# A dilated WaveNet convolution: seven wide groups in place of six, another order of blocks, and their preparation in smaller pieces

## Chip, cores and metric

One core of one Trainium2 chip. The metric is the device time of one execution in microseconds (us), the median of several runs. A profile is of one execution; its span runs from the first to the last instruction of the program, and the execution's own time is a little longer than that.

## What is computed

For two sequences of 16,000 steps with 256 channels each, a causal convolution of three taps two steps apart gives 512 channels. The first half goes through tanh, the second through a sigmoid, their product through a 256 x 256 projection. All inputs and the output are bf16.

```python
B, T, D, K = (2, 16000, 256, 3)   # x: B,T,D   w: K,D,2D   w_o: D,D
dil = 2; pad = (K - 1) * dil
xp = jnp.pad(x, ((0, 0), (pad, 0), (0, 0)))
h = einsum('btc,cd->btd', xp[:, pad:pad + T], w[0])
for i in range(1, K):
    off = pad - i * dil
    h = h + einsum('btc,cd->btd', xp[:, off:off + T], w[i])
z = jnp.tanh(h[..., :D]) * sigmoid(h[..., D:])
return z @ w_o
```

## The kernel before

**Tiles.** The 4,000 rows of four steps of each sequence are cut into groups: `groups` (lines 72 to 92), mostly 256 rows (1,024 steps), a few of 160 or 128, and `wides`, groups of 1,024 steps held as 128 rows of eight. A transposing DMA on SP brings x in with channels on partitions: `load_chunk` (line 119) loads two groups at a time into three buffers xt, `load_wide` (line 177) one wide group into two buffers xq. There are 28 plain groups (22 of 256 rows) and six wide ones, three in each sequence. The short groups stand at the end of their sequence: 160 and 128 in the middle of the order, 160, 128 and 128 at its end.

**Fewer products.** Three taps over pairs of steps are computed with fewer matmuls through sums and differences of inputs and of weights, as in a short fast-convolution. A plain block (one group and one of four output tiles of 128 channels) takes four products of two matmuls with 512 columns each: with m and p first (`products`, line 299, `which` 2 and 1), and a block later with d (3 and 0) into the same PSUM banks. Between them ScalarE copies the m product (`copy_m2`, line 338) and VectorE adds it to the p product and subtracts it (`combine`, lines 348 and 349). A wide block nests this twice: 14 matmuls of 256 columns, six at first (`wide_first`, line 232), four behind the preceding block's last products (`wide_second`, line 251) and four in the next block (`wide_last`, line 260). In between come two ScalarE copies (`wide_copies`, lines 241 and 242), two VectorE operations (`wide_sums`, line 247) and two more (`wide_combine`, lines 257 and 258).

**Who prepares.** For a plain group VectorE makes m and p (lines 278 and 284), one each in blocks of output tile 0 and 2, and GpSimd makes d, a quarter a block (`pre_d`, line 295). For a wide group GpSimd makes qa, qb and qd in six parts (`wide_part`, line 199) and, from the second group on, qp (line 214); VectorE makes qm (line 222), and for the first wide group qp also. The wide weights wf, wu and wt come in twelve VectorE steps of 256 columns, three for each output tile (line 571). `after` (line 266) makes each GpSimd operation wait for the last VectorE operation on SBUF in the same block, so that it runs beside the sums that read PSUM.

**The order.** `slots` (lines 497 to 508) lists 136 blocks: plain blocks in order, and from plain block 40 on a wide block behind every two plain ones while all neighbours belong to full groups. The loop (line 597) walks over k. In each block TensorE gets the first products of block k, the last ones of block k - 1, and one piece of the output projection (four matmuls of 256 columns, `out_mm`, line 402) if one is waiting in `todo`; in the last blocks two pieces (line 622). ScalarE gets the copy of block k, the eviction of the piece made in the preceding block (`out_evict`, line 419) and two activations of block k - 1 (`activate`, line 351). VectorE gets `combine(k)`, one of m, p or a gate (line 389), and then the weight steps and the sums of the first wide group that are due in this block. A plain group's pieces enter `todo` in the second block of the next group and may be projected two blocks later. The first wide block is block 40; its twelve half parts stand in every second block from 12 to 34, its weight steps in every second block from 9 to 31, qp in block 35 and qm in block 37. PSUM holds three buffers for each of the two banks a and b of a block, and two for the projection.

Of the kernel before, what the change touches and what calls it, by code (L numbers as in the profile page):

```python
# [9 lines left out]
ALU = mybir.AluOpType  # L10
# [3 lines left out]
def kernel(  # L14
# [57 lines left out]
    groups, chunks, wides = [], [], []  # L72
    for b in range(B):
        r0 = 0
        wide = N_WIDE[min(b, 1)]
        head, tail = sizes(FIRST if b == 0 else (), LAST[min(b, 1)], wide)
        cuts = [1, 1] if b == 0 else []
        for rs in (head, tail):
            i = 0
            while i < len(rs):  # L80
                n = cuts.pop(0) if cuts else 2
                part = rs[i:i + n]
                chunks.append((b, r0, sum(part), len(groups), len(part)))
                for r in part:
                    groups.append(dict(wide=False, b=b, r0=r0, R=r, chunk=len(chunks) - 1, col=r0 - chunks[-1][1]))
                    r0 += r
                i += n
            if rs is head:
                assert r0 > 0 and r0 % 2 == 0
                for _ in range(wide):  # L90
                    wides.append(dict(wide=True, b=b, r0=r0, R=P))
                    r0 += RG
# [93 lines left out]
    def wide_part(n, part, behind=None, qs=slice(0, 2)):  # L186
# [4 lines left out]
        if part == 0 and qs.start == 0:  # L191
            for nm in ("qa", "qb", "qd"):
                G[nm] = q_pool.tile([P, 2, 2, CT, P], bf16, name=nm)
        nm, h, in0, in1, op = (
            ("qa", 0, c[0], c[2], ALU.add), ("qb", 0, e[3], c[1], ALU.add),
            ("qa", 1, c[2], c[0], ALU.subtract), ("qb", 1, e[3], c[1], ALU.subtract),
            ("qd", 0, e[2], c[2], ALU.subtract), ("qd", 1, c[3], e[3], ALU.subtract),
        )[part]
        after(nc.gpsimd.tensor_tensor(out=G[nm][:, h, qs], in0=in0[:, qs], in1=in1[:, qs], op=op), behind)
# [10 lines left out]
    def wide_sum(n, behind=None):  # L210
        G = wides[n]
        G["qp"] = q_pool.tile([P, 2, CT, P], bf16, name="qp")
        eng = nc.gpsimd if SUM_POOL and behind else nc.vector
        ins = eng.tensor_tensor(out=G["qp"][:], in0=G["qa"][:, 0], in1=G["qb"][:, 0], op=ALU.subtract)
        if eng is nc.vector:
            return ins
        after(ins, behind)

    def wide_diff(n):
        G = wides[n]  # L220
        G["qm"] = q_pool.tile([P, 2, 2, CT, P], bf16, name="qm")
        return nc.vector.tensor_tensor(out=G["qm"][:], in0=G["qa"][:], in1=G["qb"][:], op=ALU.add)
# [9 lines left out]
    def wide_first(G, oi):  # L232
        for bank, pool in (("a", ps_a), ("b", ps_b)):
# [5 lines left out]
    def wide_copies(G, oi):  # L239
        G["ss", oi] = ss_pool.tile([P, RG], f32, name="sw")  # L240
        nc.scalar.mul(G["ss", oi][:], G["a", oi][:, RG:], 0.5)
        nc.scalar.mul(G["a", oi][:, RG:], G["a", oi][:, :RG], -1.0)
# [17 lines left out]
    def wide_last(G, oi, bank):  # L260
        if bank == "b":
# [298 lines left out]
    extra = {}  # L560
# [3 lines left out]
    def weight_steps(oi):  # L564
        o = O_ORDER[oi]
        osl = slice(o * P, (o + 1) * P)
        eng = nc.gpsimd if oi in W_POOL else nc.vector

        def tt(out, in0, in1, op):
            def step(last):  # L570
                ins = eng.tensor_tensor(out=out[:, :, osl], in0=in0[:, :, osl], in1=in1[:, :, osl], op=op)
                if eng is nc.vector:
                    return ins
                after(ins, last)
                return last
            return step

        return [
            tt(wf_sb, w_taps[2], w_taps[0], ALU.subtract),
            tt(wu_sb, wf_sb, w_taps[1], ALU.add),  # L580
            tt(wt_sb, wf_sb, w_taps[1], ALU.subtract),
        ]

    steps = [s for oi in range(4) for s in weight_steps(oi)]
    ks = [k for k in range(N_DIRECT + 2, NB) if not slots[k][0]]
    for kk, s in zip([kk for kk in ks if kk >= W_FROM][::W_STEP], steps):
        extra.setdefault(kk, []).append(s)
# [3 lines left out]
    wide_parts = {first_wide - PREP + P_STEP * i: divmod(i, 2) for i in range(12)}  # L591
# [5 lines left out]
    while k <= NB:  # L597
# [3 lines left out]
        if k < NB:  # L601
            if w:
                wide_first(G, oi)
                wide_copies(G, oi)
            else:
                products(k, 2)
                products(k, 1)
                copy_m2(k)
# [8 lines left out]
        if k < NB:  # L617
            for piece in made:
                out_evict(*piece, (not w and g == NG - 1 and oi in (0, 2)) or (len(made) > 1 and piece is made[1]))
            made = []  # L620
        second = (lambda: wide_second(G, oi)) if w else (lambda: wide_last(prev, poi, "b")) if prev["wide"] else None
        n = 0 if k in (NB - 2, NB - 1) else 2 if k > last_wide + 3 and k % 2 and unmade > NB - 1 - k else 1
# [70 lines left out]
        if k in wide_parts:  # L693
            part, q = wide_parts[k]
            wide_part(0, part, last, slice(q, q + 1))
# [9 lines left out]
    assert not todo, len(todo)  # L705
# [31 lines left out]
```

## Time and profile before

| | |
|---|---|
| runs, median (lowest to highest) | 282.95 us (282.88 to 283.25) |
| the profiled execution | 282.88 us |
| its span | 281.1 us |
| mean granted TensorE clock | 0.999 |

In the rows, PE is TensorE, PEld its weight loads, DVE VectorE, ACT ScalarE, POOL GpSimd, SP the engine that issues most DMAs. A row of the timeline has the start in us from the start of the span, the duration in us, engine, line, operation, the tile written <- the tiles read, the shape and how many were merged (x2); in brackets the idle time before it and what ended that. A row of the groups has busy time in us and the mean duration of one in ns behind the bar, then the idle time before them. A row of a stretch has its bounds and length, then for each of PE, PEld, DVE, ACT and POOL the busy time and, in brackets, the number of instructions. An operation's duration is longer than the distance at which the next one can follow, since neighbours overlap: the pace is read from starts.

### The profile page before, as it was taken

Reading aid. Unit: us, or ns where it says so; the run is one execution under the profiler, and the core shown is the slowest. Engines: PE = TensorE matmul, PEld = TensorE weight load, DVE = VectorE, ACT = ScalarE, POOL = GpSimd, SP = SyncE. Lnnn points to the kernel's source line nnn. Section 1 sums busy time; section 2 is a strip of 40 time slices with the busy share of each in tenths; the row PEclk is TensorE's granted clock in tenths of the full one; section 3 lists DMA queues with packets and bytes.
Section 4 is the critical chain, followed back from the end, with each engine's and each line's share of the span. In section 5 each row is a group of like instructions: output and inputs, shape, how many; then the busy total and the mean of one; then the engine's idle time right before and its main releaser. Section 6 shows DMA issues by size and latency. Waiting matters only on the chain.

```text
span 281.1 us, 5263 instructions
## 1 busy us (share of the span) xinstructions
PE 275.2 (98%) x1770; PEld 172.4 (61%) x1770; DVE 262.1 (93%) x477; ACT 260.5 (93%) x553; POOL 148.8 (53%) x160
## 2 busy tenths in 40 slices
PE   8999999999999999999999999999999999999994
PEld 6544555555556665765665666666666666666883
DVE  3999999999999999899999999999999999999994
ACT  5798999999999998999999999999999999999984
POOL 1145756677656663366664766575476553223320
PEclk9999999999999999999999999999999999999999
DMA  8999292642516319536269019515711711222333
GB/s 211 241 192 240 83 219 76 146 123 75 127 75 157 109 45 186 158 119 160 76 137 216 37 40 240 147 40 131 183 40 75 163 40 75 84 74 78 113 124 111
DMA packets 77979, 34.88 MB, mean 124 GB/s; under 512 B 68224, under 2 KB 70144, under 8 KB 77952
## 3 DMA queue, kind: packets, MB, share of 16 engines
q1 hardware_dynamic: 76992, 33.82, 47.4%
q10 hardware_dynamic: 960, 0.72, 0.8%
q8 instruction: 14, 0.23, 0.4%
q14 instruction: 13, 0.11, 0.1%
HBM read 1.18 MB, written 16.38 MB: 62 GB/s over the span
## 4 chain that ended last, share of the span: by engine, by line
PE 92%; DVE 4%; ACT 2%; issue 1%; DVEq 0%
PE b L314 29%; PE a L314 28%; PE o_ps L413 19%; PE a L227 9%; PE b L227 4%; PE a L115 1%; PE a L332 1%; PE b L332 1%; DVE b L348 1%; DVE b L257 1%; DVE a L349 1%; ACT ss L342 1%; ACT thw L362 0%; ACT th L372 0%; DVE mm L278 0%
## 5 line engine op out<-in xcount | busy, mean ns | idle before, releaser
L295 POOL TENSOR_TENSOR dd<-xt 128x512 bf16<-128x512 bf16 (+2 forms) x103 | 99.4, 965 | 110.3 <-DVE zz L389 41.9
L348 DVE TENSOR_TENSOR b<-a,ss 128x512 f32<-128x512 f32 (+2 forms) x108 | 70.0, 649 | 3.7 <-ACT ss L342 1.5
L349 DVE TENSOR_TENSOR a<-a,ss 128x512 f32<-128x512 f32 (+2 forms) x108 | 69.4, 642 | 0.0
L342 ACT COPY ss<-b 128x512 f32<-128x512 f32 (+2 forms) x108 | 60.3, 558 | 9.3 <-PE b L314 2.1
L314 PEld LDWEIGHTS <-wd_sb 128*128 128x128 bf16 x432 | 41.8, 98 | 40.0 <-issue 1.5
L413 PE MATMUL o_ps<-wo_sb,zz 128*128 128x256 bf16 x392 | 63.5, 272 | 0.0
L314 PE MATMUL b<-dd,wd_sb 128*128 128x512 bf16 (+2 forms) x216 | 60.4, 361 | 0.1
L314 PE MATMUL a<-dd,wd_sb 128*128 128x512 bf16 (+2 forms) x216 | 60.4, 361 | 0.0
L314 PE MATMUL a<-pp,wp_sb 128*128 128x512 bf16 (+2 forms) x216 | 60.4, 361 | 0.0
L314 PE MATMUL b<-mm,wm_sb 128*128 128x512 bf16 (+2 forms) x216 | 60.4, 361 | 0.0
L450 ACT CAST osb<-o_ps 128x512 bf16<-128x512 f32 x92 | 55.1, 599 | 0.0
L413 PEld LDWEIGHTS <-zz 128*128 128x128 bf16 x392 | 38.3, 98 | 22.2
L389 DVE TENSOR_TENSOR zz<-th,sg 128x1024 bf16<-128x1024 bf16 (+1 forms) x55 | 37.1, 677 | 0.0
L314 PEld LDWEIGHTS <-wp_sb 128*128 128x128 bf16 x216 | 21.0, 98 | 21.9 <-DVE pp L284 0.7
L372 ACT ACTIVATE sg<-b 128x512 bf16<-128x512 f32 (+2 forms) x56 | 33.0, 589 | 0.9 <-PE b L332 0.5
L372 ACT ACTIVATE th<-b 128x512 bf16<-128x512 f32 (+2 forms) x56 | 32.2, 575 | 1.6 <-PE b L314 0.8
L372 ACT ACTIVATE sg<-a 128x512 bf16<-128x512 f32 (+2 forms) x56 | 33.1, 591 | 0.0
L372 ACT ACTIVATE th<-a 128x512 bf16<-128x512 f32 (+2 forms) x56 | 32.4, 578 | 0.0
L314 PEld LDWEIGHTS <-wm_sb 128*128 128x128 bf16 x216 | 21.0, 97 | 3.5
L257 DVE TENSOR_TENSOR b<-ud,a 128x512 f32<-128x512 f32 x24 | 16.7, 696 | 5.9 <-PE a L227 3.8
L284 DVE TENSOR_TENSOR pp<-xt 128x1024 bf16<-128x1024 bf16 (+2 forms) x27 | 18.2, 673 | 0.0
L247 DVE SCALAR_TENSOR_TENSOR ud<-b,sw 128x256 f32<-128x256 f32 x48 | 17.9, 414 | 0.2
(74 smaller groups left out, 331.2 us busy)
## 6 DMA issues: line engine op xcount, KB each, us to landing
out_dram<-osb SPq DMA_DIRECT2D x60, 256.0 KB, 2.1
w_sb<-in_w_dram ACTq DMA_DIRECT2D x2, 256.0 KB, 4.2
out_dram<-osb_end SPq DMA_DIRECT2D x3, 128.0 KB, 1.9
xn<-in_x_dram SPq DMA_DIRECT2D x1, 256.0 KB, 3.0
w_sb<-in_w_dram SPq DMA_DIRECT2D x1, 256.0 KB, 4.1
xt<-in_x_dram SPq DMA_TRANSPOSE x15, 6.7
wo_sb<-in_w_o_dram ACTq DMA_DIRECT2D x1, 128.0 KB, 5.1
out_dram<-osb_odd SPq DMA_DIRECT2D x8, 16.0 KB, 2.0
```

Source lines behind the costliest of these rows:

```text
L227: nc.tensor.matmul(G[bank, oi][:, half * RG:(half + 1) * RG], lhsT=wmat[:, ct, o * P:(o + 1) * P], rhs=mv[:, :, ct, :], start=first and ct ...
L257: nc.vector.tensor_tensor(out=G["b", oi][:], in0=ud, in1=G["a", oi][:], op=ALU.subtract)
L284: return nc.vector.tensor_tensor(out=G["p"][:, :, :, :G["R"]], in0=xc, in1=yp, op=ALU.add)
L295: ins = eng.tensor_tensor(out=G["d"][:, j, :, :R], in0=a[:, q], in1=s[:, q], op=ALU.subtract)
L314: nc.tensor.matmul(G[bank, oi][:, :N], lhsT=wmat[:, ct, osl], rhs=mv(ct), start=first and ct == 0, stop=ct == CT - 1, skip_group_check=True,)
L342: nc.scalar.copy(out=G["ss", oi][:, :N], in_=G["b", oi][:, :N])
L348: nc.vector.tensor_tensor(out=pb[:, :N], in0=pa[:, :N], in1=ss[:, :N], op=ALU.subtract)
L349: nc.vector.tensor_tensor(out=pa[:, :N], in0=pa[:, :N], in1=ss[:, :N], op=ALU.add)
L372: nc.scalar.activation(out=dst[:, 2 * h:2 * h + 2, :R], in_=G[bank, oi][:, :2 * R].rearrange("p (q r) -> p q r", q=2), func=func, scale=1. ...
L389: return nc.vector.tensor_tensor(out=G["z"][:, dt, :, :full], in0=G["th"][:, dt, :, :full], in1=G["sg"][:, dt, :, :full], op=ALU.mult)
L413: nc.tensor.matmul(o_ps[:, q, :], lhsT=lhsT, rhs=wo_sb[:, dt, :], start=(dt == 0), stop=(dt == NT - 1),)
L450: copy(out=osb[:, 2 * jp:2 * jp + 2, :], in_=o_ps[:])
```

## The change

There are seven wide groups, four of them in the first sequence, and so 27 plain groups (21 of 256 rows). With `SHORT_LAST` the short groups of the first sequence go to the end of the order, ahead of those of the second: the last five groups have 160, 128, 160, 128 and 128 rows. `SPACING` says for every wide block how many plain blocks stand ahead of it: the first wide block is now block 31 and its group's others are 33, 40 and 43; from block 49 to 112 the distances repeat as 2, 1, 2, 2. Spelt out by the loop above, that is (W a wide block, its group and tile; the numbers are plain group and tile):

```
31 W0.0  32 7.3   33 W0.1  34 8.0 ... 39 9.1   40 W0.2  41 9.2  42 9.3  43 W0.3  44 10.0 ... 48 11.0
49 W1.0  50 11.1  51 W1.1  52 11.2  53 11.3  54 W1.2  55 12.0  56 12.1  57 W1.3  58 12.2  59 12.3  60 W2.0 ...
104 W6.0  105 20.0  106 W6.1  107 20.1  108 20.2  109 W6.2  110 20.3  111 21.0  112 W6.3  113 21.1 ... 135 26.3
```

The first wide group's six parts come as 24 quarters in the blocks of `P_AT` (two quarters of one half in the same block are one operation, so blocks 23 and 29 have a half), its weight steps as 24 halves in the blocks of `W_AT` (both halves in one block are one operation), all on VectorE; qp in block 19, qm in block 24. Two pieces are projected in block 126 alone; the piece evicted in blocks 9 and 129 goes to VectorE. `HOLD`, `COPIES`, `W_ENG` at these values leave the rest as it was: a wide block's two copies are still ahead of the eviction on ScalarE.

```diff
-    N_WIDE = (3, 3)
-    WIDE_FROM = 40
-    PREP = 28
-    W_FROM = 9
-    EVERY = (2,)
-    W_POOL = ()
+    N_WIDE = (4, 3)
+    SPACING = (31, 1, 6, 2, 5, 1, 2, 2, 2, 1, 2, 2, 2, 1, 2, 2, 2, 1, 2, 2, 2, 1, 2, 2, 2, 1, 2, 2,)
+    W_ENG = (0, 0, 0, 0, 0, 0, 0, 0, 0, 0, 0, 0)
+    W_AT = (6, 6, 10, 10, 14, 14, 16, 17, 18, 18, 22, 22, 24, 25, 26, 26, 28, 29, 30, 30, 34, 36, 38, 38)
+    P_AT = (7, 10, 10, 11, 12, 13, 14, 15, 16, 17, 18, 19, 20, 21, 23, 23, 23, 24, 25, 26, 27, 28, 29, 29)
+    SUM_AT, DIFF_AT = 19, 24
+    HOLD = ()
+    TWICE = (126,)
+    COPIES = 0
+    EVICT_DVE = (9, 129)
+    SHORT_LAST = True
...
+        ends.append(tail)
+        if not SHORT_LAST or b == B - 1:
+            for e in range(b + 1 if SHORT_LAST else 1):
+                add_groups(e if SHORT_LAST else b, ends[e if SHORT_LAST else b])
...
-        after(nc.gpsimd.tensor_tensor(out=G[nm][:, h, qs], in0=in0[:, qs], in1=in1[:, qs], op=op), behind)
+        after(nc.gpsimd.tensor_tensor(out=G[nm][:, h, qs, cts], in0=in0[:, qs, cts], in1=in1[:, qs, cts], op=op), behind)
...
-        if rest and i + 1 >= WIDE_FROM and since >= EVERY[(4 * len(wides) - len(rest)) % len(EVERY)] and full:
+        if rest and since >= SPACING[4 * len(wides) - len(rest)] and full:
...
-    wide_parts = {first_wide - PREP + P_STEP * i: divmod(i, 2) for i in range(12)}
+    wide_parts = {}
+    for i, kk in enumerate(P_AT):
+        wide_parts.setdefault(kk, []).append((i // 4, i % 4))
...
+            if w and COPIES == 0:
+                wide_copies(G, oi)
             for piece in made:
-                out_evict(*piece, (not w and g == NG - 1 and oi in (0, 2)) or (len(made) > 1 and piece is made[1]))
+                out_evict(*piece, (not w and g == NG - 1 and oi in (0, 2)) or (len(made) > 1 and piece is made[1]) or k in EVICT_DVE)
...
-        n = 0 if k in (NB - 2, NB - 1) else 2 if k > last_wide + 3 and k % 2 and unmade > NB - 1 - k else 1
+        n = 0 if k in (NB - 2, NB - 1) or k in HOLD else 2 if k in TWICE else 1
...
-        if k == first_wide - 5:
+        if k == SUM_AT:
             last = wide_sum(0)
-        if k == first_wide - 3:
+        if k == DIFF_AT:
             last = wide_diff(0)
 
-        for step in extra.get(k, ()):
-            last = step(last)
+        steps = extra.pop(k, [])
+        for i in sorted({i for i, _ in steps}):
+            cts = [ct for j, ct in steps if j == i]
+            last = weight_step(i, slice(cts[0], cts[-1] + 1), last)
```

More of the change, by code (lines that the diff above doesn't have):

```diff
@@ L72, with add_groups @@
     groups, chunks, wides = [], [], []
+    starts = [0] * B
+    def add_groups(b, rs, cuts=()):
+        cuts, i = list(cuts), 0
+        while i < len(rs):
+            n = cuts.pop(0) if cuts else 2
+            part = rs[i:i + n]
+            chunks.append((b, starts[b], sum(part), len(groups), len(part)))
+            for r in part:
+                col = starts[b] - chunks[-1][1]
+                groups.append(dict(wide=False, b=b, r0=starts[b], R=r, chunk=len(chunks) - 1, col=col))
+                starts[b] += r
+            i += n
+    ends = []
     for b in range(B):
-        r0 = 0
         wide = N_WIDE[min(b, 1)]
         head, tail = sizes(FIRST if b == 0 else (), LAST[min(b, 1)], wide)
[L77 to L92, printed above, removed]
+        add_groups(b, head, [1, 1] if b == 0 else [])
+        assert starts[b] > 0 and starts[b] % 2 == 0
+        for _ in range(wide):
+            wides.append(dict(wide=True, b=b, r0=starts[b], R=P))
+            starts[b] += RG
+        ends.append(tail)
+        if not SHORT_LAST or b == B - 1:
+            for e in range(b + 1 if SHORT_LAST else 1):
+                add_groups(e if SHORT_LAST else b, ends[e if SHORT_LAST else b])
+    assert starts == [T // 4] * B
     XW = max(c[2] for c in chunks)
@@ L184, in load_wide, with wide_part @@
         )
-    def wide_part(n, part, behind=None, qs=slice(0, 2)):
+    def wide_part(n, part, behind=None, qs=slice(0, 2), cts=slice(0, CT)):
         G = wides[n]
@@ L211, in wide_sum @@
         G = wides[n]
+        assert all(G["made", part] == 2 * CT for part in (0, 1))
         G["qp"] = q_pool.tile([P, 2, CT, P], bf16, name="qp")
@@ L220, in wide_diff @@
         G = wides[n]
+        assert all(G["made", part] == 2 * CT for part in (0, 1, 2, 3))
         G["qm"] = q_pool.tile([P, 2, 2, CT, P], bf16, name="qm")
@@ L232, in wide_first @@
     def wide_first(G, oi):
+        assert all(w_made.get(3 * oi + i) == CT for i in range(3))
         for bank, pool in (("a", ps_a), ("b", ps_b)):
@@ L260, in wide_last @@
     def wide_last(G, oi, bank):
+        assert all(G["made", part] == 2 * CT for part in (4, 5))
         if bank == "b":
@@ L557, with weight_step @@
     drain(groups[0], N_DIRECT + 2)
-    extra = {}
+    extra, w_made = {}, {}
     last_wide = max(k for k in range(NB) if slots[k][0])
     first_wide = slots.index((True, 0, 0))
[L564 to L587, printed above, removed]
+    for i, kk in enumerate(W_AT):
+        extra.setdefault(kk, []).append((i // 2, i % 2))
+    def weight_step(i, cts, last):
+        o = O_ORDER[i // 3]
+        sl = (slice(None), cts, slice(o * P, (o + 1) * P))
+        out, in0, in1, op = (
+            (wf_sb, w_taps[2], w_taps[0], ALU.subtract),
+            (wu_sb, wf_sb, w_taps[1], ALU.add),
+            (wt_sb, wf_sb, w_taps[1], ALU.subtract),
+        )[i % 3]
+        assert i % 3 == 0 or w_made.get(3 * (i // 3)) == CT
+        w_made[i] = w_made.get(i, 0) + cts.stop - cts.start
+        eng = nc.gpsimd if W_ENG[i] else nc.vector
+        ins = eng.tensor_tensor(out=out[sl], in0=in0[sl], in1=in1[sl], op=op)
+        if W_ENG[i]:
+            after(ins, last)
+            return last
+        return ins
     load_wide(0)
     wides_loaded = 1
-    wide_parts = {first_wide - PREP + P_STEP * i: divmod(i, 2) for i in range(12)}
+    wide_parts = {}
+    for i, kk in enumerate(P_AT):
+        wide_parts.setdefault(kk, []).append((i // 4, i % 4))
     held = []
@@ L704 @@
         k += 1
-    assert not todo, len(todo)
+    assert not todo and not extra and not wide_parts, len(todo)
     finish(made)
```

29 lines of the change are left out of this document (22 added, 7 removed).

## Prediction

> **What bounds the kernel now.** I read the page's busy times first, then the chain of work that ended last, then TensorE's instructions in order of time, and last VectorE and GpSimd where TensorE waits.
>
> ```profile
> PE 275.2 (98%) x1770; PEld 172.4 (61%) x1770; DVE 262.1 (93%) x477; ACT 260.5 (93%) x553; POOL 148.8 (53%) x160
> PE 92%; DVE 4%; ACT 2%; issue 1%; DVEq 0%
> ```
>
> The span is 281.1 us. TensorE (PE) owns 92% of the chain, but VectorE (DVE) and ScalarE (ACT) are busy for 93% each: there are three nearly full engines, and whoever falls behind stops TensorE. A busy PE says little about its pace, so I take the pace from the starts of blocks: the first matmul of a plain block reads mm, that of a wide block reads qp.
>
> ```profile
> 27.70 0.59 PE L314 MATMUL b<-mm,wm_sb 128*128 128x512 bf16 x2
> 57.99 0.38 PE L314 MATMUL b<-mm,wm_sb 128*128 128x512 bf16 x1
> 159.62 0.27 PE L227 MATMUL a<-qp,wm_sb 128*128 128x256 bf16 x1
> 184.80 0.27 PE L227 MATMUL a<-qp,wm_sb 128*128 128x256 bf16 x1
> ```
>
> The first two rows start blocks 13 and 27: 14 plain blocks in 30.29 us, 2.164 us each. The last two start blocks 78 and 90, the second blocks of wide groups 2 and 3: 8 plain and 4 wide blocks in 25.18 us, so a wide block takes (25.18 - 8 x 2.164) / 4 = 1.968 us. A wide block issues 18 matmuls of 256 columns with its piece of the output projection (14 + 4), so one costs 0.109 us; a plain block issues 8 of 512 and 4 of 256, so one of 512 costs 0.216 us.
>
> How much does TensorE lose? I count the matmuls between the starts of blocks 5 and 135.
>
> ```profile
> 11.20 0.38 PE L314 MATMUL b<-mm,wm_sb 128*128 128x512 bf16 x1
> 273.73 0.38 PE L314 MATMUL b<-mm,wm_sb 128*128 128x256 bf16 x2
> ```
>
> The code issues 700 of 512 columns, 904 of 256 and 64 of 320 there (0.136 us, between the two others): 151.1 + 98.8 + 8.7 = 258.6 us at the pace above. The rows are 262.5 us apart, so **about 4.0 us is stall**. Within this stretch a better order cannot win more than that, beyond fewer matmuls. The largest losses, as starts of neighbouring blocks:
>
> ```profile
> 22.97 0.59 PE L314 MATMUL b<-mm,wm_sb 128*128 128x512 bf16 x2
> 25.54 0.38 PE L314 MATMUL b<-mm,wm_sb 128*128 128x512 bf16 x1
> ...
> 104.29 0.27 PE L227 MATMUL a<-qp,wm_sb 128*128 128x256 bf16 x1
> 106.60 0.38 PE L314 MATMUL b<-mm,wm_sb 128*128 128x512 bf16 x1
> 108.81 0.38 PE L314 MATMUL b<-mm,wm_sb 128*128 128x512 bf16 x1
> ...
> 130.27 0.38 PE L314 MATMUL b<-mm,wm_sb 128*128 128x512 bf16 x1
> 132.29 0.38 PE L314 MATMUL b<-mm,wm_sb 128*128 128x512 bf16 x1
> ...
> 149.43 0.38 PE L314 MATMUL b<-mm,wm_sb 128*128 128x512 bf16 x1
> 151.17 0.38 PE L314 MATMUL b<-mm,wm_sb 128*128 128x512 bf16 x1
> ...
> 155.29 0.38 PE L314 MATMUL b<-mm,wm_sb 128*128 128x512 bf16 x1
> 157.46 0.38 PE L314 MATMUL b<-mm,wm_sb 128*128 128x512 bf16 x1
> ```
>
> Against its matmuls, block 11 is 0.41 late (2.57 against 2.16); block 49 0.35 (2.31 against 1.96: wide, no projection piece); block 50 0.47 (2.21 against 1.74: a plain block behind a wide one); block 64 0.28 (2.02 against 1.74); block 73 0.44 (1.74 against 1.30: no piece); block 76 0.43 (2.17 against 1.74). That is 2.38 of the 4.0. Counting the pieces through the queue of the code, blocks 48, 49, 62, 73 and 74 have none to project: TensorE runs 0.44 us ahead in each, and DVE and ACT, with nearly as much work as ever, do not follow. (43 and 54 have none either, without a loss of note.) Five of the six losses sit at these or within two blocks behind.
>
> **The change, part by part.** The sum is made against the profiled execution, 282.88 us: 281.1 of span and 1.78 around it. The median of the runs, 282.95, is 0.07 higher.
>
> *A seventh wide group.* It replaces one plain group: 32 matmuls of 512 columns go and 56 of 256 come, 6.91 - 6.12 = **0.79 us less** on the path. DVE pays more for a wide block:
>
> ```profile
> 148.75 0.74 DVE L247 SCALAR_TENSOR_TENSOR ud<-b,sw 128x256 f32<-128x256 f32 x2
> 149.60 0.70 DVE L257 TENSOR_TENSOR b<-ud,a 128x512 f32<-128x512 f32 x1
> ```
>
> The two ud operations hold it for 0.85 us, two sums of 0.60 follow, and three gates or sums of 0.60 fall on the four blocks: some 2.5 us a block. At 7 plain blocks of 1.80 (worked out below) to 4 wide ones that is 22.6 us of DVE in 7 x 2.164 + 4 x 1.968 = 23.0 of TensorE: it fits, with 0.4 to spare, so I cost it at nothing.
>
> *Short groups at the end, one wide block in 2.8.* The five short groups do the same work at the end, where the pieces (one each block, two in block 126) never run out until block 134; the last three groups and the 7.4 us behind row 273.73 stay. By the same count the new order has no piece in blocks 8 to 10 as now, then only in 35, 36, 45 and 46, each two plain blocks behind a wide one, and none from 47 to 133. So the five losses behind block 48 have lost their cause: **1.97 us less**. I put 0.2 back for 35, 36, 45 and 46 (bounds: nothing, and 0.44 each by block 73's row).
>
> *First weight step from block 9 to 6.* Block 11's loss is a wait for the sum of block 10, which stands behind that step:
>
> ```profile
> 19.05 0.70 DVE L348 TENSOR_TENSOR b<-a,ss 128x512 f32<-128x512 f32 x1 [0.18 <-ACT ss L342]
> ...
> 23.00 0.41 DVE L571 TENSOR_TENSOR wf_sb<-w_sb 128x256 f32<-128x256 bf16 x1
> 23.33 0.69 DVE L348 TENSOR_TENSOR b<-a,ss 128x512 f32<-128x512 f32 x1
> ```
>
> Taking it out starts that sum 0.33 us earlier. At block 6 it is partly covered: DVE waits 0.18 us for ACT ahead of 19.05 anyway. That leaves 0.15 of the step and the first GpSimd (POOL) piece, now in block 7, which together take back some 0.2. I take **0.13 less** (0 to 0.4). Evicting on DVE in block 9 does nothing, since no piece is made in block 8. In block 129 one eviction goes from ACT to DVE:
>
> ```profile
> L450 DVE CAST osb<-o_ps 128x512 bf16<-128x512 f32 x4 | 2.7, 684 | 0.0
> ```
>
> Four such stand among the last short blocks now and two then (another behind block 126), so I cost it at nothing.
>
> *Preparation over blocks 6 to 38.* This is the disputed part. Twelve weight steps on DVE and the first wide group's sums on POOL have to be done by block 31 for the most part, not by 40. What a POOL piece costs DVE is in these rows:
>
> ```profile
> 50.29 0.68 DVE L284 TENSOR_TENSOR pp<-xt 128x1024 bf16<-128x1024 bf16 x1
> ...
> 52.10 1.17 DVE L389 TENSOR_TENSOR zz<-th,sg 128x1024 bf16<-128x1024 bf16 x1
> ```
> ```profile
> 51.05 1.04 POOL L295 TENSOR_TENSOR dd<-xt 128x512 bf16<-128x512 bf16 x1 [0.76 <-DVE pp L284]
> 52.05 0.67 POOL L199 TENSOR_TENSOR qa<-xq 128x256 bf16<-128x256 bf16 x1
> L199 POOL TENSOR_TENSOR qa<-xq 128x512 bf16<-128x512 bf16 x10 | 11.5, 1154 | 0.0
> ```
>
> From one SBUF operation to the next DVE has pp and the two sums, three operations in 1.81 us, 0.60 each: 1.80 for a plain block. POOL's difference dd fills the two sums, which read PSUM. The half piece behind it begins 0.05 us before DVE's gate, and the gate takes 1.17 us where pp took 0.68: a half costs DVE 0.49 us. A half takes 0.67 us and a full one 1.15, so a quarter takes about 0.42 (an estimate from these two), and costs 0.49 - 0.25 = 0.24, less where POOL comes second or DVE is waiting: I take 0.20 (bounds: nothing, and the 0.49 of a half).
>
> Now DVE from block 12 to 30 of the new order: 19 blocks at 1.80 make 34.3; weight steps, five whole at 0.33 (from 23.00 to 23.33) and six halves at about 0.2, 2.9; the two sums of wide group 0 at 0.33 and 0.60, 0.9; sixteen quarters 3.2 and two halves 0.9. Together 42.2 us. TensorE needs 19 x 2.164 = 41.1. So DVE is 1.1 us late by block 31; a little of that TensorE does not feel, since DVE may fall somewhat further behind than it is at block 12, and I take **1.0 us more** (bounds: quarters at 0.13 or less, no stall; at 0.49, 4.6 us more than this). The rest of the steps, blocks 34 to 38, is 0.7 us of DVE where wide blocks stand six apart.
>
> *Transfers and the other queues.* The load of wide group 0 stays ahead of the loop; the order of chunk and wide loads on SP changes, but each later wide load is again issued in a wide group's last block, at least two plain blocks before the next group. I cost this at nothing; if one came late, POOL's sums and then a wide group's first matmuls would be late with it.
>
> **The sum:** -0.79 - 1.97 + 0.2 - 0.13 + 1.0 = -1.7 us. **282.88 - 1.7 = 281.2 us.**
>
> **The rivals.** *The quarters hide.* If POOL's quarters cost DVE 0.13 or less, the ledger above closes and the 1.0 goes: 280.2. For it: 0.05 us decides in the rows whether the piece or the gate comes first, and behind the gate a quarter would lie beside the sums. Against, with less preparation per block now:
>
> ```profile
> 37.70:81.90 44.20, 44.20 (x248) 23.86 (x247) 44.20 (x72) 42.12 (x83) 29.56 (x31) 1.00 0.43 114
> ```
>
> The third time is DVE's: busy for all of 44.2 us.
>
> *The missing pieces stall TensorE as now.* Blocks 35, 36, 45 and 46 lose 0.44 each, 1.8 in all, not 0.2: 282.8, no measurable difference. That is also what it would come to if the shorter order only moved its stalls. Against: they stand second and third behind a wide block, not at it.
>
> *The close pair.* The second block of each wide group now follows the first after one plain block, not two: seven times wide, plain, wide. ACT's copies decide there:
>
> ```profile
> 105.24 0.47 ACT L241 ACTIVATE sw<-a 128x256 f32<-128x256 f32 x1
> ...
> 147.67 0.39 ACT L241 ACTIVATE sw<-a 128x256 f32<-128x256 f32 x1
> ...
> 148.85 0.61 ACT L372 ACTIVATE th<-b 128x512 bf16<-128x512 f32 x1
> 149.34 0.62 ACT L372 ACTIVATE th<-a 128x512 bf16<-128x512 f32 x1
> ```
>
> In block 49 (start 104.29) the first copy began 0.95 us after the block, and block 49 lost 0.35; in block 72, whose successor starts at 149.43 and which takes 2.39 us, it began 0.63 after, with no loss. In the close pair I work out 0.82: ACT's four operations of 0.48 (148.85 to 149.34) exceed the plain block's 1.74 us by 0.18. If 0.82 is already too late, seven pairs at 0.35 cost 2.5 us, and with block 50's 0.47 behind each 5.7: 283.7 to 286.9, **slower**. It decides from a copy that begins some 0.9 us late. Against: the second block has no gate on DVE, and 0.1 us is left.
>
> *Pieces block for their whole length.* If a quarter, begun 0.05 us ahead, holds the gate until it ends, it costs 0.37, and sixteen of them add 2.7 us to a full DVE: 283.9; with the 0.49 of a half 285.8. Slower, from 0.34 a quarter on. Against: the half in the rows would have cost 0.62 so, and cost 0.49. The Trainium skill ("SBUF — State Buffer", Who interferes with whom) says that a VectorE operation with two SBUF inputs and a GpSimd operation that reads SBUF shut each other out for the whole instruction. By that rule this rival is what comes; the trace bears out the blocking, not its full length.
>
> **How the numbers follow.** Forecast 0.52; quarters hide 0.30; missing pieces 0.08; close pair 0.05; whole length 0.05. A measurement can tell about 0.2% (0.57 us) from no change, so faster means below 282.4 and slower above 283.5: faster 0.82, the same 0.08, slower 0.10. The range takes in the second case, down to 279.4 with 0.3 from block 11 and 0.5 from the 1.6 us of smaller losses not listed, and the missing pieces, up to 282.8.
>
> **What would show it.** Right: plain periods of 2.164 and wide ones of 1.968 throughout blocks 50 to 112, with DVE idle for almost nothing from 25 to 70 us and TensorE's blocks 12 to 31 together some 1.0 us late; POOL's quarters near 0.42 us, gates of 0.9 behind them. The first loss at block 11 shrinks to 0.2 to 0.3. Wrong: late blocks at every second wide block (the pair), or gates as long as 1.17 behind quarters, or short blocks at the end that take longer than 1.31 us (128 rows, with a piece).

## The result, and the profile after

The changed kernel takes **280.44 us** (median, 280.27 to 280.68); the kernel before, in the same comparison, 283.07. The ratio is 0.9908 with a 95% interval of 0.989 to 0.9925: faster by 0.9%. The forecast was 281.2, with a range of 279.4 to 282.8. The profiled execution took 280.49 us against 282.88. First the span, the busy times and the chain of work that ended last, from the page of the changed kernel:

```profile
span 278.7 us, 5344 instructions
...
PE 273.5 (98%) x1794; PEld 175.8 (63%) x1794; DVE 262.3 (94%) x486; ACT 260.4 (93%) x559; POOL 155.6 (56%) x173
...
PE 90%; DVE 8%; issue 1%; DVEq 0%
```

From this page little has changed: TensorE issues 24 matmuls more and is busy 1.7 us less, and VectorE has taken some of the chain from ScalarE. Where the time went is seen in the starts of blocks, in TensorE's timeline of the changed kernel (the first matmul of a plain block reads mm, that of a wide block qp; "..." marks rows left out):

```profile
11.66 0.59 PE L336 MATMUL b<-mm,wm_sb 128*128 128x512 bf16 x2
...
25.39 0.59 PE L336 MATMUL b<-mm,wm_sb 128*128 128x512 bf16 x2
...
55.68 0.59 PE L336 MATMUL b<-mm,wm_sb 128*128 128x512 bf16 x2
58.17 0.59 PE L336 MATMUL b<-mm,wm_sb 128*128 128x512 bf16 x2
...
67.06 0.38 PE L243 MATMUL a<-qp,wm_sb 128*128 128x256 bf16 x2
69.98 0.59 PE L336 MATMUL b<-mm,wm_sb 128*128 128x512 bf16 x2
72.33 0.38 PE L243 MATMUL a<-qp,wm_sb 128*128 128x256 bf16 x2
...
104.75 0.38 PE L243 MATMUL a<-qp,wm_sb 128*128 128x256 bf16 x2
...
236.49 0.38 PE L243 MATMUL a<-qp,wm_sb 128*128 128x256 bf16 x2
...
271.56 0.38 PE L336 MATMUL b<-mm,wm_sb 128*128 128x256 bf16 x2
```

These start blocks 5, 12, 26, 27, 31, 32, 33, 49, 112 and 135. From 5 to 135 it is 259.90 us. The matmuls between them need about 257.8 at the pace of the prediction, so the stall is 2.1 us; before it was about 4.0 of 262.53. Blocks 49 to 111, 40 plain and 23 wide, need 86.6 + 45.3 = 131.8 us and take 131.74: the middle of the kernel loses nothing. Block by block, the losses of the changed kernel are

| block | 6 | 10 | 11 | 26 | 28 | 31 | 32 | 41 |
|---|---|---|---|---|---|---|---|---|
| us | 0.14 | 0.07 | 0.10 | **0.32** | **0.20** | **0.53** | **0.61** | 0.09 |

Blocks 35, 36, 45 and 46, which have no piece to project, lose nothing; so do the close pairs. The four losses in bold, 1.66 us, are the end of the preparation. Two stretches there, blocks 12 to 25 and 26 to 32, each with its length and the busy time of PE, PEld, DVE, ACT and POOL:

```profile
25.40:55.68 30.28, 30.28 (x170) 16.42 (x168) 30.25 (x50) 28.55 (x57) 23.84 (x29) 1.00 0.62 142
55.68:72.33 16.65, 16.14 (x93) 8.68 (x90) 16.55 (x30) 14.71 (x30) 11.79 (x15) 1.00 0.27 84
```

VectorE is as full in the first stretch (30.25 of 30.28), which loses nothing, as in the second, which loses 1.66. A full engine is not yet a late one. How late it is shows in the distance from a block's first matmul to VectorE's first sum of that block: 1.99 us in block 12, still only 1.35 in block 24 (from 51.35 to 52.70), and 2.45 in block 25 (from 53.52 to 55.97). So VectorE does not fall behind little by little: up to block 24 it catches up. Between the sums of blocks 24 and 25, where mm, qm, half a weight step and the pieces beside them come together (the rows stand under e4), it loses 1.1 us at once, and from there to its first ud of block 31 another 1.0 (13.95 us for six blocks of 2.164).

### The profile page after: what moved, and what is told of

Its sections match the earlier page's. It is cut to its first block, busy times and chain, and to the rows that moved or that the text cites. A ratio compares the mean times of both kernels' runs of the same rounds, so it can differ in the third digit from the quotient of the medians.

```text
span 278.7 us, 5344 instructions
## 1 busy us (share of the span) xinstructions
PE 273.5 (98%) x1794; PEld 175.8 (63%) x1794; DVE 262.3 (94%) x486; ACT 260.4 (93%) x559; POOL 155.6 (56%) x173
## 4 chain that ended last, share of the span: by engine, by line
PE 90%; DVE 8%; issue 1%; DVEq 0%
PE b L336 27%; PE a L336 27%; PE o_ps L435 18%; PE a L243 11%; PE b L243 4%; DVE b L370 2%; DVE a L371 2%; PE a L354 1%; PE a L128 1%; DVE zz L411 1%; PE b L354 1%; DVE pp L306 1%; DVE wt_sb L601 0%; DVE wf_sb L601 0%; DVE qm L238 0%
## 5 line engine op out<-in xcount | busy, mean ns | idle before, releaser
L317 POOL TENSOR_TENSOR dd<-xt 128x512 bf16<-128x512 bf16 (+2 forms) x99 | 95.2, 962 | 101.8 <-DVE zz L411 32.9
L370 DVE TENSOR_TENSOR b<-a,ss 128x512 f32<-128x512 f32 (+2 forms) x104 | 67.3, 648 | 3.8 <-ACT ss L364 1.5
L371 DVE TENSOR_TENSOR a<-a,ss 128x512 f32<-128x512 f32 (+2 forms) x104 | 66.7, 641 | 0.0
L336 PE MATMUL b<-dd,wd_sb 128*128 128x512 bf16 (+2 forms) x208 | 58.0, 360 | 0.2 <-DVE b L370 0.2
L336 PE MATMUL a<-dd,wd_sb 128*128 128x512 bf16 (+2 forms) x208 | 58.0, 360 | 0.0
L336 PE MATMUL a<-pp,wp_sb 128*128 128x512 bf16 (+2 forms) x208 | 58.0, 361 | 0.0
L411 DVE TENSOR_TENSOR zz<-th,sg 128x1024 bf16<-128x1024 bf16 (+1 forms) x53 | 34.3, 649 | 0.0
L278 DVE TENSOR_TENSOR b<-ud,a 128x512 f32<-128x512 f32 x28 | 19.5, 696 | 4.0 <-PE a L243 1.9
L268 DVE SCALAR_TENSOR_TENSOR ud<-b,sw 128x256 f32<-128x256 f32 x56 | 20.9, 413 | 0.1
L435 PE MATMUL o_ps<-wo_sb,zw 128*128 128x256 bf16 x112 | 19.6, 273 | 0.0
```

Source lines behind the costliest of these rows:

```text
L268: nc.vector.scalar_tensor_tensor(out=G["ud", oi][:, h], in0=G["b", oi][:, RG:], scalar=0.5, in1=G["ss", oi][:], op0=ALU.mult, op1=op)
L278: nc.vector.tensor_tensor(out=G["b", oi][:], in0=ud, in1=G["a", oi][:], op=ALU.subtract)
L317: ins = eng.tensor_tensor(out=G["d"][:, j, :, :R], in0=a[:, q], in1=s[:, q], op=ALU.subtract)
L336: nc.tensor.matmul(G[bank, oi][:, :N], lhsT=wmat[:, ct, osl], rhs=mv(ct), start=first and ct == 0, stop=ct == CT - 1, skip_group_check=True,)
L370: nc.vector.tensor_tensor(out=pb[:, :N], in0=pa[:, :N], in1=ss[:, :N], op=ALU.subtract)
L371: nc.vector.tensor_tensor(out=pa[:, :N], in0=pa[:, :N], in1=ss[:, :N], op=ALU.add)
```

## The experiments

All are edits of the parameters of the changed kernel; e4 also adds a few lines of code. Where "..." stands in an edit, lines are left out. After each label stands the edit, then what was expected, then what came out. "Loss" is the time of a block over what its matmuls need; times are medians, and ratios are to the kernel before, run on the same chip.

**e1: only the short groups at the end.** The number of wide groups, their places and their preparation go back to what they were; one piece is projected in every block to the end, where the kernel before has two in some of the last blocks.

```diff
-    N_WIDE = (4, 3)
-    SPACING = (31, 1, 6, 2, 5, 1, 2, 2, ...)
-    W_AT = (6, 6, 10, 10, 14, 14, 16, 17, ...)
-    P_AT = (7, 10, 10, 11, 12, 13, ...)
-    SUM_AT, DIFF_AT = 19, 24
-    TWICE = (126,)
-    EVICT_DVE = (9, 129)
+    N_WIDE = (3, 3)
+    SPACING = (40,) + (2,) * 23
+    W_AT = (9, 9, 11, 11, ..., 31, 31)
+    P_AT = (12, 12, 14, 14, ..., 34, 34)
+    SUM_AT, DIFF_AT = 35, 37
+    TWICE = ()
+    EVICT_DVE = ()
```

> The kernel before with one part of the change alone: the short groups of the first sequence moved to the end, one piece projected in every block to the end, no eviction moved; six wide groups from block 40 on, every third block, preparation where it was. By count only blocks 43, 48 and 49 then have no piece to project. Theory A (TensorE loses its time where no piece is left to project and VectorE and ScalarE cannot follow): the 0.8 us of blocks 49 and 50 stay, the 1.15 of blocks 64, 73 and 76 and some 0.5 of the short blocks go: 283.0 - 1.65 = 281.4 us (281.1 to 281.8). Rival B (the gain came from the seventh group and the earlier start, and the losses merely go elsewhere): 283.0 within 0.3.

Measured 281.37 us, 0.9937 (0.9914 to 0.996). Blocks 11, 49 and 50 lose 0.40, 0.35 and 0.48 as they did; the losses behind block 50, of blocks 64, 73, 76 and 97 and of the short blocks at the end, are gone but for 0.16 in the last blocks. So this order, with one piece in each of the last blocks, brings about two thirds of what the whole change brings.

**e4: no pieces on GpSimd.** The first wide group's parts are not made; its tiles are set to zero ahead of the loop, so that group's output leaves out its input.

```diff
-    P_AT = (7, 10, 10, 11, 12, 13, ...)
+    P_AT = ()
+        wides[0][nm] = q_pool.tile([P, 2, 2, CT, P], bf16, name=nm)
+        nc.gpsimd.memset(wides[0][nm][:], 0.0)
...
```

> The changed kernel without GpSimd's sums of the first wide group, whose tiles are set to zero at the start (that group's output leaves out its input). Theory A (GpSimd's pieces and VectorE's weight steps together overfill VectorE before block 31): the losses of blocks 26, 28, 31 and 32, 1.7 us, go: 278.8 (278.5 to 279.2). Rival B (the weight steps and the first wide block's own waits make them): less than 0.5 of it goes, 279.9 or more.

Measured 278.87 us, 0.9855 (0.9838 to 0.9873), and blocks 26, 28, 31 and 32 lose nothing. The weight steps stand where they stood, and the same VectorE operations are short. VectorE's timeline around block 26, first of the changed kernel, then of e4:

```profile
43.48 0.93 DVE L411 TENSOR_TENSOR zz<-th,sg 128x1024 bf16<-128x1024 bf16 x1
...
52.70 0.69 DVE L370 TENSOR_TENSOR b<-a,ss 128x512 f32<-128x512 f32 x1
...
53.90 1.13 DVE L300 TENSOR_TENSOR mm<-xt 128x1024 bf16<-128x1024 bf16 x1
54.96 0.88 DVE L238 TENSOR_TENSOR qm<-qa,qb 128x1024 bf16<-128x1024 bf16 x1
55.77 0.28 DVE L601 TENSOR_TENSOR wf_sb<-w_sb 128x128 f32<-128x128 bf16 x1
55.97 0.68 DVE L370 TENSOR_TENSOR b<-a,ss 128x512 f32<-128x512 f32 x1
...
68.54 1.12 DVE L306 TENSOR_TENSOR pp<-xt 128x1024 bf16<-128x1024 bf16 x1
69.58 0.41 DVE L601 TENSOR_TENSOR wf_sb<-w_sb 128x256 f32<-128x256 bf16 x1
69.92 0.74 DVE L268 SCALAR_TENSOR_TENSOR ud<-b,sw 128x256 f32<-128x256 f32 x2
70.76 0.70 DVE L278 TENSOR_TENSOR b<-ud,a 128x512 f32<-128x512 f32 x1
```
```profile
54.14 0.69 DVE L305 TENSOR_TENSOR mm<-xt 128x1024 bf16<-128x1024 bf16 x1
54.74 0.68 DVE L243 TENSOR_TENSOR qm<-qa,qb 128x1024 bf16<-128x1024 bf16 x1
55.34 0.29 DVE L606 TENSOR_TENSOR wf_sb<-w_sb 128x128 f32<-128x128 bf16 x1
...
67.12 0.69 DVE L311 TENSOR_TENSOR pp<-xt 128x1024 bf16<-128x1024 bf16 x1
```

The pieces that stood beside them in the changed kernel, on POOL:

```profile
43.44 0.43 POOL L213 TENSOR_TENSOR qa<-xq 128x128 bf16<-128x128 bf16 x1
...
53.85 0.63 POOL L213 TENSOR_TENSOR qb<-xq 128x256 bf16<-128x256 bf16 x1
54.44 0.85 POOL L213 TENSOR_TENSOR qd<-xq 128x128 bf16<-128x128 bf16 x1
...
68.50 0.61 POOL L213 TENSOR_TENSOR qd<-xq 128x256 bf16<-128x256 bf16 x1
```

A quarter of 0.43 us that begins 0.04 ahead of the gate makes the gate 0.93 in place of the 0.68 that gates take in e4; a half of 0.63, 0.05 ahead of mm, makes it 1.13. That is 0.25 and 0.45, about 0.18 less than the piece lasts. Most quarters do cost what the prediction said, and do not hide. A few cost nothing: the one at 48.03, behind a gate that begins at 47.93, has two sums after it, and the first of them begins 0.62 us after the gate.

**e2: halves in place of quarters**, and **e3: six wide groups in place of seven**, the order otherwise as in the change.

```diff
-    P_AT = (7, 10, 10, 11, 12, 13, ...)
+    P_AT = (7, 7, 9, 9, 11, 11, ..., 29, 29)
```
```diff
-    N_WIDE = (4, 3)
+    N_WIDE = (3, 3)    # and the last group's four distances cut from SPACING
```

> The changed kernel with the first wide group's sums as twelve halves in every second block from 7 to 29 in place of the smaller pieces. Theory A (a piece costs VectorE its time beyond the sums that read PSUM: 0.49 us a half, 0.24 a quarter, so twelve halves cost 5.9 and the twenty quarters and two halves 5.8): 280.4 within 0.4, blocks 12 to 32 lose 1.2 to 2.2 us. Rival B (small pieces are what lets the preparation fit): at least 1 us slower, 281.4 or more.

> The changed kernel with six wide groups in place of seven, the order otherwise the same up to block 101. Theory A (TensorE sets the pace from block 44 on, so the seventh group is worth its matmuls): 0.79 us more, 281.2 (281.0 to 281.5). Rival B (VectorE sets the pace in the wide stretch, so fewer matmuls save nothing there): 280.4 within 0.2, or less.

e2 measured 280.9 us, 0.9928 (0.9909 to 0.9947), between the two answers. Blocks 26 to 32 lose 1.36 in place of 1.66, but blocks 11 and 12, now beside halves, lose 0.35 and 0.47 and blocks 20 to 24 another 0.2. So the halves spare VectorE nothing: 0.3 less is lost there, and some 0.9 more ahead of it.

e3 measured 281.81 us, 0.9956 (0.9944 to 0.9968), with a spread of 281.42 to 282.38; that is above both answers (the first reached to 281.5). In its trace the matmuls need 0.79 more, as expected, blocks 26 to 32 lose the same, and only block 5 differs much, by 0.36. Of the 1.4 us between the two medians 0.8 is thus the seventh group; where the other 0.6 comes from is open (block 5's 0.36 can be a part of it).

**e7: wide blocks at every third place**, and **e8: the close pair moved by one wide block**, so that its second block is the group's third.

```diff
-    SPACING = (31, 1, 6, 2, 5, 1, 2, 2, 2, 1, 2, 2, ...)
+    SPACING = (31,) + (2,) * 27
```
```diff
-    SPACING = (31, 1, 6, 2, 5, 1, 2, 2, 2, 1, 2, 2, ...)
+    SPACING = (31, 1, 6, 2, 5, 2, 1, 2) + (2, 2, 1, 2) * 5
```

In e7 half a weight step also moved from block 34 to 35, since 34 is now a wide block.

> The changed kernel with the wide blocks at even distance, every third block from 31 to 112 with no close pair (step 10 in blocks 35 and 36). Theory A (the close pair costs nothing; a block without a piece costs about 0.44 us where it stands directly behind a wide block): blocks 35 and 41 now stand so, and 0.7 to 0.9 us is added there: 281.2 us (280.9 to 281.6), with no change from block 49 on. Rival B (the close pairs cost something that the even order saves): 280.4 or less.

> The changed kernel with the close pair of wide groups 1 to 6 moved from their first and second block to their second and third, where VectorE has a gate in the third. Theory A (the pair is free only where its second block has no gate): in the third block VectorE's sum starts 2.76 us after the block's start in place of 2.57, so each of six pairs loses about 0.2: 1.2 us more, 281.6 (281.2 to 282.0). Rival B (a close pair is free anywhere): 280.4 within 0.2.

e7 measured 282.61 us, 0.9988 (0.9974 to 1.0002), worse than either answer. It loses 2.1 us more in blocks 35 to 44 and nothing from 49 on. So the close pair is no cost, and the prediction's empty blocks cost nothing because they stand two or three behind a wide block: put directly behind one, as blocks 35 and 41 here, they cost 0.24 and 0.74. (The profiled execution, 281.9, is 0.7 below the median; that rest is open.)

e8 measured 281.75 us, 0.9956 (0.9942 to 0.9969). Each of the six moved pairs loses 0.20 or 0.21, everything else as in the change. The first of them, blocks 54 to 56 on TensorE, and the sum of wide block 54 on VectorE:

```profile
115.10 0.38 PE L243 MATMUL a<-qp,wm_sb 128*128 128x256 bf16 x2
117.49 0.59 PE L336 MATMUL b<-mm,wm_sb 128*128 128x512 bf16 x2
119.43 0.59 PE L336 MATMUL b<-mm,wm_sb 128*128 128x512 bf16 x2
```
```profile
117.87 0.70 DVE L278 TENSOR_TENSOR b<-ud,a 128x512 f32<-128x512 f32 x1
```

Block 55 takes 1.94 us where its matmuls need 1.74, and the sum of block 54 began 117.87 - 115.10 = 2.77 us after its block. This is the number that ties the cases together, below.

**e5: the weight steps of the other output tiles later**, behind the first wide block, and wide block 2 one place later; **e6: the first wide block at 34**, with all pieces single quarters; **e9 and e11: the weight steps moved alone**, e9 partly ahead of the first wide block, with qm in block 27, e11 behind it as e5, but in the order of the change.

```diff
e5  SPACING = (31, 1, 6, 3, 4, 1, 2, 2, ...)
e5  W_AT = (6, 6, 10, 10, 14, 14, 16, 17, 18, 18, 22, 22, 32, 32, 34, 34, 37, 37, 30, 30, 38, 38, 41, 41)
e6  SPACING = (34, 1, 4, 2, 4, 1, 2, 2, ...)
e6  W_AT = (6, 6, 10, 10, 14, 14, 18, 18, 22, 22, 26, 26, 30, 30, 32, 32, 35, 35, 37, 37, 38, 38, 42, 42)
e6  P_AT = (7, 10, 11, 12, ..., 31, 32)
e6  SUM_AT, DIFF_AT = 19, 27
e9  W_AT = (..., 22, 22, 23, 23, 25, 25, 32, 32, 30, 30, 34, 34, 38, 38)
e9  SUM_AT, DIFF_AT = 19, 27
e11 W_AT = (..., 22, 22, 28, 28, 32, 32, 34, 34, 30, 30, 37, 37, 38, 38)
```

> The changed kernel with weight steps 6 to 8 (counted from 0) moved from blocks 24 to 29 to blocks 32, 34 and 37, step 10 from 34 and 36 to 38, step 11 from 38 to 41, and the fourth wide block from 43 to 44. Theory A (VectorE is overfilled by some 1.5 us ahead of block 31, and any 1.1 us taken out of blocks 24 to 30 comes back on TensorE): the losses of blocks 26 to 32, 1.7 us, fall to 0.6 and nothing of note is added behind: 279.4 us (279.1 to 279.8). Rival B (only GpSimd's pieces matter, since a run without them lost nothing with all weight steps in place): less than 0.4 is won, 280.0 or more.

> The changed kernel with the first wide group at blocks 34, 36, 41 and 44 in place of 31, 33, 40 and 43; its pieces as 24 single quarters in block 7 and blocks 10 to 32, weight steps whole in blocks 6, 10, 14, 18, 22, 26, 30, 32, 35, 37, 38 and 42, the second sum in block 27. Theory A (the ledger of VectorE: 22 blocks from 12 to 33 hold 47.4 us of work in 47.6 of TensorE's): the losses of 1.7 us ahead of the first wide blocks shrink to under 0.5, some 0.2 is lost at blocks 39 to 41: 279.2 us (278.9 to 279.8). Rival B (the first wide block itself costs what blocks 31 and 32 lose, wherever it stands): 1.1 us stays there, 280.0 or more.

> The changed kernel with weight steps 6, 7 and 8 in blocks 23, 25 and 32 (whole), step 10 whole in block 34, and wide group 0's second sum in block 27 in place of 24; the order of blocks untouched. Theory A (the losses ahead of block 33 are one overfull stretch of VectorE, so it is enough to spread the same work by the room that each block has): of the 1.7 us some 0.1 stays at block 31, nothing is added: 278.9 us (278.7 to 279.3). Rival B (the wide start itself has a price that only a later fourth wide block or fewer pieces takes away): 279.6 or more.

> The changed kernel with its order of blocks untouched (fourth wide block at 43, second sum in block 24) and weight steps 6 to 11 whole in blocks 28, 32, 34, 30, 37 and 38: as in the run with later weight steps, but with one step back ahead of block 31 and none behind block 40. Theory A (room on VectorE block by block): block 26 loses 0.13 as there, block 31 or 32 some 0.2, blocks 36, 37 and 41 together 0.4, block 45 nothing since it no longer stands directly behind a wide block: 279.1 us (278.9 to 279.5). Rival B (the order of the balanced run's miss: anything added ahead of block 31 comes back whole): block 32 loses 0.5 or more, 279.6 or more.

| | us | ratio (95%) | stall, 5 to 135 | losses that remain |
|---|---|---|---|---|
| e5 | 279.22 | 0.9866 (0.984 to 0.9891) | 1.14 | 26 0.13, 41 0.23, 45 0.37 |
| e6 | 280.15 | 0.99 (0.9875 to 0.9925) | 1.77 | 41 0.28, 42 0.44, 45 0.74 |
| e9 | 279.87 | 0.9881 (0.9865 to 0.9896) | 1.39 | 29 0.18, 32 0.59 |
| e11 | 279.37 | 0.987 (0.9853 to 0.9888) | 1.38 | 5 0.37, 26 0.14, 36 0.15, 41 0.23 |

e5 and e11 came out as expected and beat the change by 1.0 to 1.2 us. So the pieces need not go, as in e4: it is enough to take two or three weight steps out of the way. e6's time is outside the first answer and in the second's, but not for the reason given there: ahead of block 34 and at it nothing is lost but the 0.31 of blocks 6 to 11, as the first answer had it. It loses behind: two weight steps ahead of wide block 41, and block 45, without a piece, now directly behind wide block 44. e5 made the same mistake at block 45, for less; TensorE's rows of it for blocks 31 to 33 and 44 to 46, and the sum of block 44:

```profile
66.48 0.38 PE L243 MATMUL a<-qp,wm_sb 128*128 128x256 bf16 x2
68.88 0.59 PE L336 MATMUL b<-mm,wm_sb 128*128 128x512 bf16 x2
70.61 0.38 PE L243 MATMUL a<-qp,wm_sb 128*128 128x256 bf16 x2
...
93.51 0.38 PE L243 MATMUL a<-qp,wm_sb 128*128 128x256 bf16 x2
95.90 0.59 PE L336 MATMUL b<-mm,wm_sb 128*128 128x512 bf16 x2
97.57 0.59 PE L336 MATMUL b<-mm,wm_sb 128*128 128x512 bf16 x2
```
```profile
96.01 0.70 DVE L278 TENSOR_TENSOR b<-ud,a 128x512 f32<-128x512 f32 x1
```

The first two blocks take 2.40 and 1.73, no loss; block 45 takes 1.67 where its matmuls need 1.30.

e9 missed its first answer: block 32 still loses 0.59. It leaves more work ahead of block 31 than e11 does, and qm stands in block 27. TensorE's rows of e9 for blocks 31 to 33, then VectorE's and POOL's:

```profile
66.94 0.38 PE L243 MATMUL a<-qp,wm_sb 128*128 128x256 bf16 x2
69.39 0.59 PE L336 MATMUL b<-mm,wm_sb 128*128 128x512 bf16 x2
71.72 0.38 PE L243 MATMUL a<-qp,wm_sb 128*128 128x256 bf16 x2
```
```profile
67.95 0.69 DVE L306 TENSOR_TENSOR pp<-xt 128x1024 bf16<-128x1024 bf16 x1
68.56 0.83 DVE L601 TENSOR_TENSOR wf_sb<-w_sb 128x256 f32<-128x256 bf16 x1
...
70.16 0.70 DVE L278 TENSOR_TENSOR b<-ud,a 128x512 f32<-128x512 f32 x1
```
```profile
68.05 1.06 POOL L213 TENSOR_TENSOR qd<-xq 128x256 bf16<-128x256 bf16 x1
```

And VectorE's in e11, whose block 31 starts at 66.51:

```profile
66.92 0.69 DVE L306 TENSOR_TENSOR pp<-xt 128x1024 bf16<-128x1024 bf16 x1
67.53 0.83 DVE L601 TENSOR_TENSOR wf_sb<-w_sb 128x256 f32<-128x256 bf16 x1
...
69.12 0.70 DVE L278 TENSOR_TENSOR b<-ud,a 128x512 f32<-128x512 f32 x1
```

In both pp comes first and takes its 0.69, the piece waits (its record reads 1.06 for the 0.61 of the same half in the change), and the weight step behind pp pays: 0.83 in place of 0.41. By these rows and the one at 48.03 above, a piece that comes second is free only if VectorE's next operation is not one on SBUF. The difference between e9 and e11 is how late VectorE already is: pp begins 1.01 us after the block in e9, 0.41 in e11.

**e10 and e12: the changed kernel and e5 once more.**

> The changed kernel itself once more, beside the balanced one on the same chip: 280.4 us within 0.3; its losses at blocks 26, 28, 31 and 32 the same to 0.02 us if they come from the order of the work and not from chance.

> The run with later weight steps once more, beside this one on the same chip: 279.2 us within 0.3, block 45 loses 0.37 again.

e10 measured 280.36 us, 0.9904 (0.9887 to 0.9921), e12 279.41, 0.987 (0.9849 to 0.989). In e10 blocks 26, 28, 31 and 32 lose 0.32, 0.20, 0.52 and 0.61, the same to 0.01: these losses are set by the program, not by chance.

## Why the prediction was right, and which step was off

**One number decides at a wide block.** Take how long after the block's first matmul VectorE begins its sum (b<-ud). In the changed kernel's blocks 54 to 104, undisturbed, it is 2.56 or 2.57 in most and never more. So it is in wide block 109, here with the start of block 111 and the sum of block 109:

```profile
230.20 0.38 PE L243 MATMUL a<-qp,wm_sb 128*128 128x256 bf16 x2
...
234.33 0.59 PE L336 MATMUL b<-mm,wm_sb 128*128 128x512 bf16 x2
```
```profile
232.77 0.70 DVE L278 TENSOR_TENSOR b<-ud,a 128x512 f32<-128x512 f32 x1
```

The sum begins 2.57 us after the block, and blocks 109 and 110 take 4.13 us, what their matmuls need. Whatever comes later is lost in full, in that block and the next; if one of the two has no piece to project, the limit is 0.44 earlier, 2.13 (four matmuls of 0.109).

| kernel, wide block | sum after start | limit | over | lost |
|---|---|---|---|---|
| change, 31 | 3.70 | 2.57 | 1.13 | 0.53 + 0.61 |
| e9, 31 | 3.22 | 2.57 | 0.65 | 0.06 + 0.59 |
| e11, 31 | 2.61 | 2.57 | 0.04 | 0.05 |
| e8, 54 | 2.77 | 2.57 | 0.20 | 0.20 |
| e7, 37 | 3.44 | 2.57 | 0.87 | 0.23 + 0.64 |
| e5, 44 (no piece behind) | 2.50 | 2.13 | 0.37 | 0.37 |
| e6, 44 (no piece behind) | 2.86 | 2.13 | 0.73 | 0.74 |
| before, 75 | 3.01 | 2.57 | 0.44 | 0.43 |
| before, 96 | 2.91 | 2.57 | 0.34 | 0.35 |
| before, 49 (no piece in it) | 2.96 | 2.13 | 0.83 | 0.35 + 0.47 |

The prediction did not know this limit. Step by step it compares so:

| step, in the profiled executions | forecast | measured |
|---|---|---|
| seventh wide group | -0.79 | -0.79 |
| five losses behind block 48 | -1.97 | -1.97 |
| blocks 35, 36, 45, 46 | +0.2 | 0 |
| block 11 | -0.13 | -0.31 |
| **preparation** | **+1.0** | **+1.66** |
| block 97; short blocks at the end with blocks 33, 47, 56, 59 and smaller ones | 0 | -0.35; -0.67 |
| start-up and block 5; blocks 10 and 41 | 0 | +0.09; +0.16 |
| behind the start of block 135 | 0 | -0.23 |
| sum | -1.7 | -2.4 |

*The seventh group and the order* were right in mechanism and size. e1 shows that the losses leave without the seventh group and the earlier start; the 0.79 of that group is a count of matmuls, which e3's trace bears out, though its time came out higher. The close pair fits, as the prediction argued, because its second block has no gate: its sum begins 2.37 after the start. ScalarE's first copy begins 0.82 us after block 51, just as the prediction worked out, and nothing is lost. In e8 it begins 0.82 after block 54 as well, and there 0.20 is lost, as much as VectorE's sum is over the limit. So a price of the pair exists, 0.2 and not 0.35 to 0.82, and it comes from VectorE's sum, not from the copy that the rival named.

*The empty blocks* are the prediction's second rival, and it fell as argued, by their place. But e5, e6 and e7 show that the price is real where the empty block stands directly behind the wide one; the 0.44 of the prediction is the whole shift of the limit, paid only when the sum is later than 2.13.

*The preparation* is the step that was mis-sized, 1.0 against 1.66: "DVE is 1.1 us late by block 31; a little of that TensorE does not feel ... and I take 1.0 us more." VectorE, hardly ever idle, took 42.54 us from the sum of block 12 (at 27.38) to the first ud of block 31 (at 69.92); the forecast said 42.2, and TensorE's 19 blocks need 41.12. The prediction then allowed VectorE a little more lag than at block 12. In fact the sum of block 12 stood 27.38 - 25.39 = 1.99 behind its block, while ud of a wide block may be 2.57 - 0.84 = 1.73 behind: VectorE has to be 0.26 *nearer*. 42.54 - 41.12 + 0.26 = 1.68, which is what TensorE lost. Of the 0.66 about 0.34 is work, 0.26 is this limit, and the rest the lag that the prediction allowed. Most of the 0.34 is the pieces: read from starts, VectorE's operations beside them take some 4.4 us longer in this stretch than they do undisturbed (an estimate), where the prediction had 4.1. The ledger took the 19 blocks as one sum; block by block, as shown above, VectorE catches up 0.6 us until block 24 and falls 2.1 behind from there, half of it in that one block.

*The quarters* cost 0.25 in the rows where the prediction worked out 0.24, so the first rival (they hide) fell, by e4 as well. The fourth rival, blocking for the whole length, fell by the same rows: 0.25 of 0.43, 0.45 of 0.63. The Trainium skill ("SBUF — State Buffer", SBUF: two separate sides) has the two operations shut each other out for the whole instruction; the trace bears out that they exclude each other, in e9 in the other direction too, but the delay is some 0.18 us shorter than the piece.

*What the sum left out* is the larger error, 1.0 us of smaller losses counted as staying. The short blocks at the end lost some 0.4 us with two pieces in some blocks, and lose next to nothing with one. Block 97's 0.35 came from one wait of VectorE in the kernel before:

```profile
200.30 0.70 DVE L257 TENSOR_TENSOR b<-ud,a 128x512 f32<-128x512 f32 x1 [0.46 <-PE o_ps L413]
```

With it the sum of block 96 is 0.34 over the limit, which is the loss. The operation does not read the projection's o_ps, whose matmuls ended about 0.36 us ahead of it, so the releaser named is not the cause; with the new order the wait is gone, and what it was stays open. Two errors, +0.66 and about -1.4, partly cancelled: the forecast was 0.8 too high, in the range and on the right side.

## What to carry to other kernels

When several engines are nearly full, busy shares do not tell which is late; measure how far the follower runs behind the leader at each block, find the largest lag that costs nothing (here 2.57 us), and spread extra work so that no block passes it. A block with spare independent work behind a dependent one is worth as much as that work is long. Work that is needed only later should not stand ahead of the tightest point: taking two weight steps from ahead of the first wide block to places behind it, with two others moved back (e11), brought 1.0 us more where the whole change had brought 2.6.

## What the runs showed that was not expected

The start varies. The first matmuls on x sometimes run slowly; the first six into bank a, in the changed kernel and in the kernel before:

```profile
4.99 1.34 PE L354 MATMUL a<-xt,w_sb 128*128 128x256 bf16 x6
```
```profile
4.84 0.82 PE L332 MATMUL a<-xt,w_sb 128*128 128x256 bf16 x6 [0.22 <-ACT xt L169]
```

Over all profiled executions block 5 starts between 10.95 us (e7) and 12.13 us (e10, the changed kernel itself). When it starts between 11.0 and 11.3, block 5 itself loses 0.35 to 0.37 (e2, e3, e8, e11 and the kernel before), so part of it evens out, but e7, at 10.95, loses nothing there. No experiment was made on the cause of either, and differences of up to 0.5 us between two profiles can come from here alone: e10 ran 0.47 us longer than the first profile of the same kernel, and its block 5 started 0.47 later.
